# Sliding-window attention and MLP on one core: head pairs 10 and 11 moved from the early to the late kind of attention, and a new order of the first two blocks' slices

## The chip, the cores and the metric

The kernel runs on one core of a Trainium2 chip. The metric is the device time of one execution in microseconds (us); lower is better. Most executions of one kernel agree within 0.3%.

## What is computed

Attention over 4 batches of 8 heads, 768 positions and head size 64, with a band of 96 keys, 8 global keys and a distance bias; then a two-layer MLP (512 to 2048 to 512) on all 3072 tokens, in float32.

```python
scores = scale * np.matmul(q, k.transpose(0, 1, 3, 2))
is_global = pos[None, :] < int(n_global)
is_local = (rel >= 0) & (rel < int(n_local))
keep = is_global | is_local
scores = scores - slopes[:, None, None] * dist[None, :, :]
scores = np.where(keep, scores, -1000000000.0)
a = np.exp(scores - np.max(scores, axis=-1, keepdims=True))
a = a / (np.sum(a, axis=-1, keepdims=True) + 1e-09)
x = np.matmul(a, v)           # then heads side by side: 3072 x 512
h = x @ w_in
g = h * np.clip(h + 3.0, 0.0, 6.0) / 6.0
out = g @ w_out
```

## The kernel before

**Blocks, pairs, slices.** The tokens form 8 blocks of 384 (half a sequence each). A block's attention is done in 4 pairs of heads, so pair n belongs to block n // 4: pairs 0 to 3 to block 0, 4 to 7 to block 1, 8 to 11 to block 2. A block's MLP is done in 16 slices of the hidden layer (f = 0 to 15). A slice has two halves on TensorE: `first` (12 matmuls, L166, into a bank of `hp`) and `second` (9 matmuls, L198, into the block's three accumulators). Between them ScalarE adds 3 and clips below (`g`, L177), VectorE finishes the gate (L178), and the product is split into a high part (`gh`, L186 on ScalarE or L184 on GpSimd) and a rest (`gl`, L191 on VectorE). TensorE does the first half of the next slice before the second half of the last one. Each float32 product is made of three such reduced matmuls (high x high, low x high, high x low), hence 12 and 9.

**The weights** arrive as 64-bit floats, as 32 chunks of two 32-bit words each: chunk 2f holds the slice f of the first layer, chunk 2f + 1 that of the second. `decode` turns each into a high and a low part: on VectorE the steps L393, L394, L402 (merges the high word), L408 (adds the low word) and L399 (the low part, `w1l` or `w2l`); on ScalarE L371 and L412; on GpSimd L375 (`we`). Only two raw chunks fit, so the load of chunk i + 2 (L363, on SyncE's queue) is issued after L402 of chunk i. `work` gives out decode steps against a running account of TensorE time; `decoded_to` forces those that a slice needs.

**Two kinds of attention.** The early kind (`plain`) is for the time in which the weights aren't there: scores are full float32 matmuls (L809 or L813), VectorE adds the distances and takes the least (L824), ScalarE exponentiates (L828), VectorE sums and inverts (L838, L839), GpSimd normalises (L848), TensorE transposes (`turn`, L856 and L858), ScalarE or VectorE copies the transposes out (L860), and `values` multiplies (L900); `put_x` splits the result (L152 on ScalarE, L153 on VectorE). Before the change, pairs 0 to 9 have both heads side by side (`both`), and pairs 10 and 11 are still early but in a third form with one bank and operands of 128 rows. The late kind splits queries and keys (`split`: L783 on ScalarE, L784 on GpSimd, L787 and L790 on VectorE), takes scores with four reduced matmuls for each of three tiles (L813), transposes on VectorE (`spread`, L873), and carries the blocks over DRAM and back (L875 writes `there`, L882 reads `weights`, both on SyncE's queue); TensorE does only scores and `values`. The late kind is laid between the halves of a block's slices: `attention` returns a list of units, and unit k runs after the k-th half.

**Order of the work.** TensorE, GpSimd and SyncE keep the order in which the program issues (`in_order`); the other engines are put in order by the scheduler. First come pairs 0 to 11 in the loop over n, with block 0's slices 0 to 5 (`FIRST = 6`) fed in from n = 8. Then block 1's slices 0 to 5, then the slices 6 to 15 of blocks 0 and 1 in turns, all without attention beside them. From block 2 on, each block's slices carry the late attention of the block after. Block 1's sums lie in the three banks of the pools `ps_s`, `ps_t`, `ps_x`, block 0's in the three of `ps_o`.

Of the kernel before, what the change touches and what calls it, by code (L numbers as in the profile page):

```python
# [20 lines left out]
NT = 3  # L21
# [21 lines left out]
AHEAD = 3  # L43
EARLY = AHEAD * NPAIR
BOTH = 10
# [4 lines left out]
FIRST = 6  # L50
# [8 lines left out]
class Kernel:  # L59
# [222 lines left out]
    def place(self, n):  # L282
        return self.room[n % (MORE if n < EARLY else ROOMS)]

    def load(self, n, values):

        if n < len(self.blocks) * NPAIR:
            end = KW + (TB if n < BOTH else QW)
            for columns in (slice(KW + QW, LOAD),) if values else (slice(0, KW), slice(KW, end)) if n == 0 else (slice(0, end),):
                self.nc.sync.dma_start(out=self.place(n)[:, columns], in_=self.pairs[n, :, columns])  # L290

    def load_next(self, n, values):

        if n < EARLY - MORE + ROOMS:
            self.load(n + MORE, values)
        elif n >= EARLY:
            self.load(n + ROOMS, values)
# [181 lines left out]
    def banded(self, flag):  # L479
# [7 lines left out]
        self.turn, self.more, self.score_banks = {}, True, 1  # L487
# [4 lines left out]
        with ExitStack() as early, ExitStack() as words:  # L492
# [5 lines left out]
            def decoded_all():  # L498
                words.close()
                self.op = self.pool("op", 2, ctx=early, side="right")  # L500

            self.decoded_all = decoded_all
# [4 lines left out]
            with ExitStack() as ctx:  # L507
# [10 lines left out]
                def half():  # L518
                    if not self.more:
                        next(todo, None)  # L520

                for n in range(-2, EARLY + 1):
                    if n + 2 < NPAIR:
                        self.distances(n + 2)
                    if n == 8:
                        self.more = False
                        acc.extend(self.acc_tiles())
                    if n + 2 < BOTH:
# [9 lines left out]
                    for t in range(NT):  # L538
                        if n + 2 < EARLY:
                            if n + 2 < BOTH:  # L540
# [42 lines left out]
        self.score_banks = 2  # L583
        self.op = self.pool("op", 3, side="right")
        x, ahead = xs[2], None
# [30 lines left out]
    def attention(self, i, x, first):  # L616

        units = [[] for _ in range(2 * NF - 2)]
        pairs = [first or Pair(self, i * NPAIR, x, False)]
        pairs[0].x = x  # L620
        if first is None:
            for k in range(3):
                pairs[0].split(k, False)
            units[1].append(lambda: self.load_next(pairs[0].n, False))
        for p in range(NPAIR):
            n = i * NPAIR + p
            me, after = pairs[p], Pair(self, n + 1, x, False) if n + 1 < len(self.blocks) * NPAIR else None
            pairs.append(after)
            at = units[6 * p:]
            for t in range(NT):  # L630
                at[t].append(lambda t=t, me=me: me.scores(t)())
            if after:
                at[3].append(lambda after=after: after.split(0))
# [3 lines left out]
            for t in range(1, NT if after else 0):  # L637
                at[t + 3].append(lambda t=t, after=after: after.split(t))
            if p % 2 == 1:
                at[11] += [lambda me=pairs[p - 1]: me.values("x"), lambda me=me: me.values("s")]  # L640
        return units, pairs[NPAIR]
# [112 lines left out]
class Pair:  # L754
# [4 lines left out]
    def __init__(self, kernel, n, x, plain):  # L759
        self.k, self.nc, self.n, self.x, self.plain, self.both = kernel, kernel.nc, n, x, plain, n < BOTH  # L760
# [34 lines left out]
    def scores(self, t):  # L795
# [3 lines left out]
        if t != 1 or not self.both:  # L799
            self.banks = [kk.bank("s")[:, 0:2 * W].rearrange("p (i c) -> p i c", i=2) for _ in range(2 if self.both else 1)]  # L800
        sp = [self.banks[j][:, t % 2] if self.both else self.banks[0][:, j] for j in range(2)]
# [4 lines left out]
        for j in range(2):  # L806
            if self.plain:
                rows, q = (slice(j * D, (j + 1) * D), 0) if self.both else (slice(None), j)
                nc.tensor.matmul(sp[j][:, lo:W], lhsT=queries[rows, q, t], rhs=keys[rows, c], start=True, stop=True)  # L809
# [40 lines left out]
    def turn(self, t):  # L850
# [9 lines left out]
        (nc.vector.tensor_copy if kk.more and t == 1 else nc.scalar.copy)(out=pt[:, :, c], in_=tp[:, :, c])  # L860
# [61 lines left out]
def pair_loads(q, k, v):  # L922
# [8 lines left out]
    for b in range(B):  # L931
        for a in range(0, S, TB):
            cols = np.concatenate([np.arange(a - PREV, a).clip(0)]
                                  + [np.concatenate([np.arange(NG), np.arange(p, p + P)]) for p in range(a, a + TB, P)])
            for h in range(0, H, 2):
# [3 lines left out]
                for j in range(2):  # L939
                    for half in range(2):  # L940
                        if n >= EARLY or half == j:
                            column = KW + (j * TB if n >= BOTH else 0)
# [37 lines left out]
```

## Time and profile before

| What | before |
|---|---|
| median of 3 runs | 668.01 us (667.44 to 668.05) |
| the profiled execution's own time | 668.19 us |
| its span, first to last instruction | 666.4 us |
| mean granted TensorE clock | 0.999 |
| first matmul of block 0's slice 0 | at 51.55 us |
| first matmul of block 2's slice 0 (the 33rd slice) | at 202.72 us |
| VectorE busy | 423.4 us (64%) |
| ScalarE busy | 278.9 us (42%) |
| GpSimd busy | 219.9 us (33%) |
| moved by DMA | 84.74 MB |

A page of the profile gives busy time by engine over the span; the timeline gives single instructions (start, length, engine, line, operation, and in brackets the idle time before it and what ended that). On VectorE and TensorE neighbouring instructions overlap, so what one costs is read from the start of one to the start of the next. The time outside the span is 1.79 us.

### The profile page before, as it was taken

How to read it: one execution, taken by the hardware profiler on the slowest of the kernel's cores; microseconds unless marked ns; L12 is line 12 of the kernel's file. 1: busy time of each engine (PE TensorE's matmuls, PEld its weight loads, DVE VectorE, ACT ScalarE, POOL GpSimd, SP SyncE). 2: the span in 40 equal slices, each digit the busy share in tenths (PEclk: the TensorE clock that was granted, in tenths of full speed). 3: DMA queues.
4: the chain of work that ended last, by engine and by line, in shares of the span. 5: the costliest groups of instructions: out<-in, count | busy, mean ns of one | idle time of the engine just before them, and what ended most of it. 6: DMA issues, size and time to landing. Idle time of an engine off the chain costs nothing.

```text
span 666.4 us, 11474 instructions
## 1 busy us (share of the span) xinstructions
PE 654.5 (98%) x3963; PEld 586.1 (88%) x3963; DVE 423.4 (64%) x1121; ACT 278.9 (42%) x736; POOL 219.9 (33%) x389
## 2 busy tenths in 40 slices
PE   9989999999999999999999999999999999999997
PEld 8768888888999999999999999899999999989995
DVE  6899999999234876366663886457662777422222
ACT  6898756555236333154324433143331444131111
POOL 5666622221000553043340444225340444302110
PEclk9999999999999999999999999999999999999999
DMA  8685644442003446625663366624555255510001
GB/s 288 179 253 195 198 150 135 153 134 94 1 1 134 135 139 184 174 81 138 164 154 131 86 179 164 173 80 126 155 152 137 80 150 147 138 48 2 1 1 53
DMA packets 60837, 84.74 MB, mean 127 GB/s; under 512 B 8416, under 2 KB 45536, under 8 KB 60768
## 3 DMA queue, kind: packets, MB, share of 16 engines
q1 hardware_dynamic: 60480, 83.64, 43.3%
q8 instruction: 33, 0.54, 0.3%
q14 instruction: 36, 0.29, 0.1%
q10 hardware_dynamic: 288, 0.26, 0.1%
HBM read 62.92 MB, written 20.97 MB: 126 GB/s over the span
## 4 chain that ended last, share of the span: by engine, by line
PE 81%; DVE 9%; ACT 3%; DMA 3%; issue 2%; POOL 1%; SPq 0%; ACTq 0%; DVEq 0%; POOLq 0%
PE hp L166 36%; PE acc L198 33%; DMA wst<-w 3%; PE xp L900 2%; PE sp L813 2%; PE tp L900 2%; PE tp L813 2%; ACT n L828 2%; DVE wz L402 2%; DVE wz L408 1%; DVE n L824 1%; DVE wz L394 1%; PE sp L198 1%; PE tp L198 1%; PE xp L198 1%
## 5 line engine op out<-in xcount | busy, mean ns | idle before, releaser
L177 ACT ACTIVATE g<-hp,small 128x384 f32<-128x384 f32 x127 | 73.5, 579 | 251.5 <-PE hp L166 231.9
L166 PE MATMUL hp<-xh,w1h 128*128 128x384 f32 x512 | 174.1, 340 | 0.8 <-ACT w1h L412 0.7
L166 PE MATMUL hp<-xh,w1l 128*128 128x384 f32 x512 | 172.9, 338 | 0.1
L166 PE MATMUL hp<-xl,w1h 128*128 128x384 f32 x512 | 172.0, 336 | 0.0
L184 POOL TENSOR_SCALAR gh<-g 128x384 fp32r<-128x384 f32 x96 | 51.6, 538 | 292.6 <-DVE g L178 257.4
L198 PE MATMUL acc<-w2h,gl 128*128 128x512 f32 x336 | 133.0, 396 | 0.1
L198 PE MATMUL acc<-w2l,gh 128*128 128x512 f32 x336 | 132.4, 394 | 0.0
L198 PE MATMUL acc<-w2h,gh 128*128 128x512 f32 x336 | 132.0, 393 | 0.0
L178 DVE SCALAR_TENSOR_TENSOR g<-g,hp 128x384 f32<-128x384 f32 x128 | 69.7, 544 | 86.7 <-ACT g L177 86.5
L848 POOL TENSOR_SCALAR n<-n,sums 128x232 f32<-128x232 f32 (+1 forms) x186 | 101.7, 562 | 35.7 <-DVE sums L839 21.3
L191 DVE TENSOR_TENSOR gl<-g,gh 128x384 fp32r<-128x384 f32 x128 | 78.6, 614 | 50.0 <-POOL gh L184 45.3
L828 ACT ACTIVATE n<-n,least 128x232 f32<-128x232 f32 (+1 forms) x192 | 89.1, 466 | 45.1 <-DVE least L824 43.9
L166 PEld LDWEIGHTS hp<-xh,w1h 128*128 128x128 f32 x512 | 96.3, 188 | 6.6 <-issue 1.4
L166 PEld LDWEIGHTS hp<-xl,w1h 128*128 128x128 f32 x512 | 96.2, 188 | 3.9
L166 PEld LDWEIGHTS hp<-xh,w1l 128*128 128x128 f32 x512 | 96.0, 188 | 0.4 <-DVE w1l L399 0.4
L198 PEld LDWEIGHTS acc<-w2h,gl 128*128 128x128 f32 x336 | 63.0, 187 | 14.7 <-DVE gl L191 1.0
L198 PEld LDWEIGHTS acc<-w2h,gh 128*128 128x128 f32 x336 | 63.3, 188 | 10.3 <-POOL gh L184 0.3
L198 PEld LDWEIGHTS acc<-w2l,gh 128*128 128x128 f32 x336 | 63.2, 188 | 10.3
L873 DVE STREAM_TRANSPOSE blocks<-n 128x256 f32<-128x256 f32 x112 | 43.5, 424 | 31.0 <-POOL n L848 18.7
L375 POOL TENSOR_SCALAR we<-wst 128x512 int32<-128x512 uint32 x32 | 27.8, 868 | 68.6 <-DMA wst<-w 52.2
L784 POOL TENSOR_SCALAR kx<-load 64x504 fp32r<-64x504 f32 (+1 forms) x40 | 31.0, 776 | 37.5 <-PE hp L166 35.9
L824 DVE CUSTOM_DVE_ANT_0 n<-sp,d 128x232 f32<-128x232 f32 (+1 forms) x70 | 23.6, 374 | 29.5 <-PE sp L813 29.0
(110 smaller groups left out, 780.9 us busy)
## 6 DMA issues: line engine op xcount, KB each, us to landing
wst<-w SPq DMA_DIRECT2D x32, 512.0 KB, 3.5
load<-pairs SPq DMA_DIRECT2D x22, 636.0 KB, 5.2
there<-blocks SPq DMA_DIRECT2D x52, 256.0 KB, 2.6
load<-pairs SPq DMA_DIRECT2D x32, 384.0 KB, 3.9
weights<-there SPq DMA_DIRECT2D x48, 192.0 KB, 3.8
out<-o SPq DMA_DIRECT2D x23, 256.0 KB, 2.1
weights<-there SPq DMA_DIRECT2D x32, 160.0 KB, 3.2
load<-pairs SPq DMA_DIRECT2D x9, 444.0 KB, 3.6
```

What stands on the lines that cost most here:

```text
L166: self.nc.tensor.matmul(hp, lhsT=self.w1(w, f)[:, kt, :], rhs=a[:, kt, :], start=(n == 0), stop=(n == 3 * NKT - 1))
L177: nc.scalar.activation(out=g, in_=hp, func=AF.Relu, bias=self.three, scale=1.0)
L178: nc.vector.scalar_tensor_tensor(out=g, in0=g, scalar=6.0, in1=hp, op0=ALU.min, op1=ALU.mult)
L184: self.nc.gpsimd.tensor_scalar(out=gh, in0=g, scalar1=1.0, scalar2=0.0, op0=ALU.mult, op1=ALU.add)
L191: self.nc.vector.tensor_tensor(out=gl, in0=g, in1=gh.bitcast(F32), op=ALU.subtract)
L198: self.nc.tensor.matmul(acc[tt], lhsT=a[:, tk], rhs=self.w2(w, f), start=(f == 0 and j == 0), stop=(f == NF - 1 and j == 2))
L375: self.nc.gpsimd.tensor_scalar(out=self.e[i], in0=words[:, :, 0].bitcast(U32), scalar1=2.0 ** -29, scalar2=0.0, op0=ALU.mult, op1=ALU.add)
L784: nc.gpsimd.tensor_scalar(out=part["kx"][own, c], in0=k[own, c], scalar1=1.0, scalar2=0.0, op0=ALU.mult, op1=ALU.add)
L824: nc.vector.tensor_tensor_reduce(out=e[:, j, lo:W], in0=sp[j][:, lo:W], in1=d, op0=ALU.add, op1=ALU.min, scale=scale, scalar=3.0e38, accum ...
L828: nc.scalar.activation(out=e[:, j, lo:W], in_=e[:, j, lo:W], func=AF.Exp, bias=self.least[:, i:i + 1], scale=-1.0, accum_out=self.sums[:, ...
L848: nc.gpsimd.tensor_scalar(out=e[:, j, lo:W], in0=e[:, j, lo:W], scalar1=over, scalar2=0.0, op0=ALU.mult, op1=ALU.add)
L873: nc.vector.transpose(out=blocks[:, :, s].rearrange("p b j q -> p j b q"), in_=e[:, :, c:c + P].rearrange("p j (b q) -> p j b q", b=4))
```

## The change

Three things are changed together.

1. The early kind ends at pair 9 (`EARLY = 10`), and its third form is gone. Pairs 10 and 11 get the late kind. They are laid beside block 1's slices 8 to 15, with the new argument `begin`, in which a pair takes 5 units where it otherwise takes 6, and the two pairs' `values` come at unit 15, after the second half of block 1's slice 14. Their scores and values use the banks of `ps_o` (stage "one"), which block 0 leaves.
2. Of block 0, 3 slices (`FIRST = 3`) are in the loop of the early attention, not 6. The rest follows in the order of the string `ORDER`, a digit for a slice's block: 13 slices of block 0 (3 to 15) among 8 of block 1 (0 to 7), so that block 0 is done before block 1's slice 8 has its second half.
3. The loads follow: pairs from 10 on are loaded into two places, with an index shifted by one.

```diff
-EARLY = AHEAD * NPAIR
-BOTH = 10
+EARLY = 10
-FIRST = 6
+FIRST = 3
+ORDER = "101001010010010100100"
...
     def place(self, n):
-        return self.room[n % (MORE if n < EARLY else ROOMS)]
+        return self.room[n % MORE if n < EARLY else (n + 1) % ROOMS]
...
-        pools = {"s": (s, o, o, o), "t": (t, h, h), "x": (x,)}[what] if self.more else {"s": (s, t)[:self.score_banks], "t": (t,), "x": (x,)}[what]
+        pools = {"attention": {"s": (s, o, o, o), "t": (t, h, h), "x": (x,)}, "both": {"t": (t,), "x": (x,)},
+                 "one": {"s": (o,), "x": (o,)}, "layers": {"s": (s, t), "t": (t,), "x": (x,)}}[self.stage][what]
...
                         if n + 2 < EARLY:
-                            if n + 2 < BOTH:
-                                weigh[t]()
-                            else:
-                                pairs[n + 2].scores(t)()
-                                if t == NT - 1:
-                                    self.load_next(n + 2, False)
-                            self.work(0 if n + 2 < BOTH else 0.78, 0.64)
+                            weigh[t]()
+                            self.work(0, 0.64)
...
-            todo = [(1, f, xs[1], acc1) for f in range(FIRST)]
-            todo += [(i, f, xs[i], (acc, acc1)[i]) for f in range(FIRST, NF) for i in range(2)]
+            next_f, todo = [FIRST, 0], []
+            for block in map(int, ORDER):
+                todo.append((block, next_f[block], xs[block], (acc, acc1)[block]))
+                next_f[block] += 1
             for _ in self.halves(todo):
                 pass
+            self.decoded_to(2 * NF - 1)
...
+        self.stage = "one"
+        units, ahead = self.attention(2, xs[2], Pair(self, EARLY, xs[2], False), True)
+        for k, _ in enumerate(self.halves([(1, f, xs[1], acc1) for f in range(next_f[1], NF)], True)):
+            for unit in units[k]:
+                unit()
+        self.stage = "layers"
...
-            at = units[6 * p:]
+            at = units[5 * p + 1 if begin else 6 * p:]
...
-            if p % 2 == 1:
-                at[11] += [lambda me=pairs[p - 1]: me.values("x"), lambda me=me: me.values("s")]
+            if n % 2 == 1:
+                at[9 if begin else 11] += [lambda me=pairs[p - 1]: me.values("x"), lambda me=me: me.values("s")]
```

On VectorE, where the early attention ends, these rows stood after pair 8's normalisation was prepared: L838 and L839 are pair 9's sums, L824 pair 10's distances, L402, L408 and L399 the decode of chunk 3, L178 slice 0's gate.

```order
L838 TENSOR_SCALAR sums<-sums 128x6
L824 ISA n,least<-sp,p_176 128x128
L824 ISA least 128x1
L824 ISA n,least<-sp,p_176 128x128
L824 ISA least 128x1
L839 RECIPROCAL sums<-sums 128x6
L402 SCALAR_TENSOR_TENSOR wz<-wst,wz 128x512
L153 TENSOR_TENSOR xl<-xp,xh 128x384
L408 ISA wz<-wz,we 128x1024
L178 SCALAR_TENSOR_TENSOR g<-g,hp 128x384
```

The same place on VectorE after the change (the line numbers are one lower from L165 on).

```order
L837 TENSOR_SCALAR sums<-sums 128x6
L402 SCALAR_TENSOR_TENSOR wz<-wst,wz 128x512
L838 RECIPROCAL sums<-sums 128x6
L152 TENSOR_TENSOR xl<-xp,xh 128x384
L408 ISA wz<-wz,we 128x1024
L177 SCALAR_TENSOR_TENSOR g<-g,hp 128x384
L399 TENSOR_TENSOR w2l_143<-wz,w2h_142 128x512
L393 TENSOR_SCALAR wz<-wz 128x512
L190 TENSOR_TENSOR gl<-g,gh 128x384
```

Pair 10's distances are gone from between them, as pair 11's are a little later, and the decode steps move up.

On TensorE, at the end of block 1 in the program before, block 1's last second half (into `sp`, `tp`, `xp`) follows the first half of block 2's slice 0, and then come the scores of pair 12.

```order
L198 MATMUL tp<-w2h_1393,gl 128x512
L198 MATMUL xp<-w2h_1393,gh 128x512
L198 MATMUL xp<-w2l_1394,gh 128x512
L198 MATMUL xp<-w2h_1393,gl 128x512
L813 MATMUL sp<-kx,q_2409 128x232
L813 MATMUL sp<-kx,q_2410 128x232
```

After the change, at the same place on TensorE: the second half of block 1's slice 14, then the values of pairs 10 and 11, then the first half of block 2's slice 0.

```order
L197 MATMUL xp<-w2h_1102,gl 128x512
L899 MATMUL acc<-weights,load_73 64x128 x10
L899 MATMUL acc<-weights,load_72 64x128 x10
L165 MATMUL hp<-xh,w1h_140 128x384
L165 MATMUL hp<-xl,w1h_140 128x384
```

Block 2's last two value products now stand directly ahead of the first matmuls that read block 2's `x`.

More of the change, by code (lines that the diff above doesn't have):

```diff
@@ L518, in half @@
                 def half():
-                    if not self.more:
+                    if self.stage == "both":
                         next(todo, None)
@@ L632, in attention @@
             if after:
-                at[3].append(lambda after=after: after.split(0))
+                at[2 if begin else 3].append(lambda after=after: after.split(0))
             at[3] += [me.sum_up, lambda me=me: me.normalize(0), lambda me=me: me.normalize(1)]
@@ L637, in attention @@
             for t in range(1, NT if after else 0):
-                at[t + 3].append(lambda t=t, after=after: after.split(t))
-            if p % 2 == 1:
-                at[11] += [lambda me=pairs[p - 1]: me.values("x"), lambda me=me: me.values("s")]
-        return units, pairs[NPAIR]
+                at[t + (2 if begin else 3)].append(lambda t=t, after=after: after.split(t))
+            if n % 2 == 1:
+                at[9 if begin else 11] += [lambda me=pairs[p - 1]: me.values("x"), lambda me=me: me.values("s")]
+        return units, pairs[-1]
     def general_setup(self):
@@ L807, in scores @@
             if self.plain:
-                rows, q = (slice(j * D, (j + 1) * D), 0) if self.both else (slice(None), j)
-                nc.tensor.matmul(sp[j][:, lo:W], lhsT=queries[rows, q, t], rhs=keys[rows, c], start=True, stop=True)
+                rows = slice(j * D, (j + 1) * D)
+                nc.tensor.matmul(sp[j][:, lo:W], lhsT=queries[rows, 0, t], rhs=keys[rows, c], start=True, stop=True)
             else:
```

51 lines of the change are left out of this document (23 added, 28 removed).

## Prediction

> **What bounds the kernel now.** I read the page first, then busy time in stretches, then the chain of waits, then the timelines of TensorE and VectorE up to 166 us. The page:
>
> ```profile
> span 666.4 us, 11474 instructions
> PE 654.5 (98%) x3963; PEld 586.1 (88%) x3963; DVE 423.4 (64%) x1121; ACT 278.9 (42%) x736; POOL 219.9 (33%) x389
> ```
>
> TensorE is the bound on the average. The stretches (start and end; then busy us of PE, PEld, DVE, ACT, POOL; clock; DMA share; GB/s) tell where something else is close:
>
> ```profile
> 51.00:78.00 27.00, 26.19 (x188) 23.17 (x189) 25.87 (x69) 22.48 (x61) 18.47 (x26) 1.00 0.63 198
> 78.00:97.00 19.00, 17.39 (x115) 14.80 (x115) 17.55 (x34) 11.07 (x21) 4.79 (x5) 1.00 0.52 165
> 97.00:162.40 65.40, 65.31 (x326) 58.27 (x325) 64.76 (x122) 38.71 (x67) 16.29 (x18) 1.00 0.41 137
> ```
>
> From 51 to 162 us VectorE (DVE) is as full as TensorE (PE): the rows sum to 108.2 of 111.4 us, against 108.9. It decodes the weights there. After 97 us TensorE hardly waits for that, because the program before gives it slices of block 1 that need no new weights. So the change meets two full engines, and I count both and take the later. The chain gives what a slice costs, what the late kind adds to TensorE, and a mark at 165.16 us:
>
> ```profile
> 160.96 2.12 PE hp L166 x12
> 165.16 2.10 PE hp L166 x12
> ...
> 311.07 0.39 PE sp L813 x4
> 313.58 0.45 PE tp L813 x4
> 316.13 0.44 PE sp L813 x4
> 322.85 1.25 PE xp L900 x20
> 324.10 1.10 PE tp L900 x20
> ```
>
> A slice is 165.16 - 160.96 = 4.20 us, a half 2.1. A late pair of a sequence's first half, as 10 and 11 are, takes 0.39 + 0.45 + 0.44 = 1.28 us for scores, and two such pairs 2.35 us for values: 4.9 us for both. The mark is the 24th first half, since of the matmuls that occur four times in a slice 92, for 23 slices, begin before it:
>
> ```profile
> L166 PE MATMUL hp<-xl,w1h x92: 334/337/342, 51.8 to 162.6; 128*128 128x384 f32 x92
> ```
>
> **The change, part by part.** *TensorE up to the mark.* The 24th first half follows 3 + 20 slices now (it is the last digit of `ORDER`, block 0's slice 15), 6 + 17 before. Nothing differs up to about 51 us. From there:
>
> ```profile
> 51.55 0.45 PE L166 MATMUL hp<-xh,w1h 128*128 128x384 f32 x1
> 53.77 0.95 PE L809 MATMUL sp<-load 128*128 128x232 f32 x4
> 54.55 0.27 PE L856 MATMUL tp<-ident,n 128*128 128x128 f32 x1
> 55.08 1.54 PE L900 MATMUL xp<-pt,load 128*64 128x128 f32 x24
> 56.55 1.05 PE L809 MATMUL sp<-load 128*128 128x232 f32 x4
> ```
>
> From start to start: a first half 2.2 us, a tile's scores 0.78, four transposes 0.5, values 1.47; a second half is 2.1 as above. Out go pairs 10's and 11's six tiles of scores (4.7 us), their transposes and their values, and three slices are put off. Left are 3 first halves (6.6), 2 second (4.2), five groups of transposes (2.5 at most, one of them half as long) and the values of pairs 7 to 9 (4.4 at most): 17.0 to 17.7 us. So block 1's first slice can begin at 68.5 to 69.2 us and the mark, 20 slices of 4.20 later, at 152.5 to 153.2 us as far as TensorE goes.
>
> *VectorE up to the mark.* The mark needs chunk 30, whose last step is the fourth row here:
>
> ```profile
> 52.92 0.17 DVE L838 TENSOR_SCALAR sums<-sums 128x6 f32<-128x6 f32 x1
> 127.17 0.55 DVE L178 SCALAR_TENSOR_TENSOR g<-g,hp 128x384 f32<-128x384 f32 x1
> 127.63 0.69 DVE L408 CUSTOM_DVE_ANT_0 wz<-wz,we 128x1024 uint16<-128x1024 uint16 x1
> 162.38 0.68 DVE L399 TENSOR_TENSOR w1l<-wz,w1h 128x512 fp32r<-128x512 f32 x1
> ```
>
> And these are groups of the 65.0 us from 97.3 to 162.3:
>
> ```profile
> L408 DVE CUSTOM_DVE_ANT_0 wz<-wz,we 128x1024 uint16<-128x1024 uint16 x18 | 15.0, 836 | 0.3
> L191 DVE TENSOR_TENSOR gl<-g,gh 128x384 fp32r<-128x384 f32 x16 | 9.7, 604 | 0.0
> L178 DVE SCALAR_TENSOR_TENSOR g<-g,hp 128x384 f32<-128x384 f32 x15 | 8.1, 543 | 0.0
> ```
>
> A gate takes 127.63 - 127.17 = 0.46, say 0.47, and I give a rest as much; 31 of them 14.6; so each of 18 chunks takes (65.0 - 14.6) / 18 = 2.80 us. In the new order, from 52.92 us to chunk 6's last step: 3.5 chunks (9.8), three gates and rests (2.8), three splits of `x` of a gate's size (1.4), sums and their like (1.1): 68.0 us. From there to chunk 30's: 24 chunks (67.2), 20 gates and rests (18.8), one split (0.5): 154.5 us. The mark can begin 0.3 us later, since only its third matmul reads that low part: 154.8. Pairs 10's and 11's work on VectorE is gone from this count. It has no idle time but that after 97 us; from 51 to 97 us VectorE idled 27.00 - 25.87 + 19.00 - 17.55 = 2.6 us in the rows above. The decode still has one load on its way per chunk, so I keep half, 1.3 us: 156.1 us. VectorE is the later by some 3 us, and TensorE will wait about that much for weights, which it hardly does now after 97 us. The mark comes 165.16 - 156.1 = 9.1 us earlier.
>
> *After the mark* the slices are the same in number. Added is the late work of two pairs, 4.9 us on TensorE, with nothing to hide it. Its part on VectorE (splits, distances, transposes) comes behind the last chunk, so it delays no weights. On SyncE's queue block 0's three stores now stand ahead of pair 12's load and of pair 10's `there`, and no weight load is left behind them.
>
> *A new wait.* Pair 11's values stand 7 halves, one score group and pair 10's values behind the start of its last scores: 14.7 + 0.45 + 1.25 = 16.4 us. By then its blocks must have been over DRAM. Two pairs of this form before: the start of their last scores, their reads' issue on SyncE's queue, and from issue to landing (least, median, most):
>
> ```profile
> 288.21 0.61 PE L813 MATMUL sp<-kx,q 128*128 128x232 f32 x4
> 302.71 1.76 SPq L882 DMA_DIRECT2D weights<-there  x4
> DMA to landing us min/median/max: 2.6/3.3/3.9
> ...
> 302.09 0.61 PE L813 MATMUL tp<-kx,q 128*128 128x232 f32 x4
> 314.70 1.73 SPq L882 DMA_DIRECT2D weights<-there  x4
> DMA to landing us min/median/max: 2.6/3.2/3.6
> ```
>
> The last of four reads is issued about 1.3 us after the first (three quarters of 1.76): landed at 302.71 + 1.3 + 3.9 = 307.9, or 314.70 + 1.3 + 3.6 = 319.6, that is 19.7 or 17.5 us after the scores began. These pairs have 6 units each and time enough; with 5, TensorE stands for 1.1 to 3.3 us, and queued behind are block 2's first half and all the rest. I take 1.7, nearer to the second, a pair that is the odd one of its two as 11 is. [...] The banks that blocks 0 and 1 leave to scores cost some tenths, since a store's scaling ends about when the second half does: 0.3 in all, 0 to 1.
>
> *The sum*: -9.1 + 4.9 + 1.7 + 0.3 = -2.2 us on the span. The profiled execution took 668.19, so 666.0 from it; the median of the runs lies 0.18 lower and gives 665.8 us.
>
> **The rivals.** *The decode goes slower than counted, and the kernel with it (slower).* Weights landed late where pair loads ran beside them:
>
> ```profile
> 74.43 4.64 DMA wst<-w
> 83.42 3.42 DMA wst<-w
> ```
>
> The new order asks for chunks 5 to 10 sooner. If each of the ten chunks from 4 on loses half of the 1.22 us between these two, that is 6 us of idle VectorE: 671.9 us. It decides from 2.2 us of such idle time on. For it: VectorE's idle time from 78 to 97 us. Against: no pair's load but part of pair 11's is left for that time (its values), and by the counts the decode leads at chunk 6 (68.0 us, wanted only two halves after 68.5).
>
> *Pair 11's blocks are later still.* At the 19.7 us of the first pair the wait is 3.3 us, and with a microsecond more for the stores on the queue 4.3: 668.4 us, no change.
>
> *GpSimd sets VectorE free, and TensorE stays the bound.* Beside POOL's `we` VectorE's merges take longer:
>
> ```profile
> 73.48 0.68 DVE L402 SCALAR_TENSOR_TENSOR wz<-wst,wz 128x512 int32<-128x512 int32 x1
> 81.76 1.14 DVE L402 SCALAR_TENSOR_TENSOR wz<-wst,wz 128x512 int32<-128x512 int32 x1
> 71.47 5.09 POOL L848 TENSOR_SCALAR n<-n,sums 128x128 f32<-128x128 f32 x6 [0.17 <-ACT wz L371]
> 81.36 0.99 POOL L375 TENSOR_SCALAR we<-wst 128x512 int32<-128x512 uint32 x1 [1.47 <-DMA wst<-w]
> ```
>
> 0.46 us is lost beside 0.99 of POOL. If the normalisation of pairs 10 and 11, 5.09 us for one of them, costs VectorE at that rate, 4.7 us come free when it leaves this stretch, the mark falls to TensorE's 152.5, and the time to 662.2. Against: the merge at 73.48 ran beside such a normalisation and kept its 0.68. [...]
>
> *That the change doesn't do what it says* is no case here: the orders above show both pairs moved.
>
> **How the numbers follow.** A measurement of this kernel tells about 0.2% (1.3 us) from no change. Chances: the forecast 0.55, slow decode 0.12, late blocks 0.23, free VectorE 0.10. Within the forecast's case the mark may lie from 154.8 to 157.5 and the waits from 0.5 to 2.5; one part in six of it is within 0.2%. Faster: 0.46 + 0.10 = 0.56. Slower: most of the slow decode and a fifth of the late blocks, 0.15. Same: 0.29. The low end has the mark at 154.8 and half a microsecond of waits: 665.8 - 1.3 - 1.5 = 663.0. The high end has late blocks and 1.6 us of late weights: 668.4 + 1.6 = 670.0.
>
> **What would show it.** Right: the 24th first half at 155 to 157 us; between 69 and 156 us waits of PE for `w1h` or `w1l` of 3 to 5 us in all; VectorE full up to 157; and 1 to 3 us of idle PE ahead of the second values of L899 in `acc`, which stand near 198 us. Wrong: a mark beyond 158.3 us, which eats the gain; VectorE idle while weights are awaited; or more than 4 us in front of those values.

## The result and the profile after

The changed kernel takes 672.16 us (median of 6 runs, 671.80 to 674.87), the kernel before 668.02 in 6 runs beside it: a ratio of 1.0077, 95% interval 1.0058 to 1.0096. It is slower by 4.1 us, where the forecast was 665.8 and faster. The profiled execution took 672.15 us, near the median. A few executions, four of the kernel before and one of e10_chain, took far longer (799 to 3664 us); every ratio in this document leaves them out.

The page of the changed kernel, first the totals, then the granted clock in 40 slices of the span:

```profile
span 670.3 us, 11482 instructions
...
PE 653.7 (98%) x3943; PEld 582.6 (87%) x3943; DVE 433.5 (65%) x1139; ACT 274.9 (41%) x726; POOL 221.0 (33%) x401
...
PEclk9999999998999999999999999999999999999999
```

TensorE is a shade less busy than before (653.7 us, 654.5 before) and the span is 3.9 us longer, so TensorE waits more. One slice has an 8 in the clock, where the page before has none. The stretches (columns as before: busy us of PE, PEld, DVE, ACT, POOL; clock; DMA share; GB/s):

```profile
51.00:78.00 27.00, 26.63 (x186) 23.65 (x185) 24.32 (x48) 17.61 (x38) 9.38 (x15) 1.00 0.59 179
78.00:97.00 19.00, 18.68 (x92) 16.11 (x92) 18.73 (x36) 11.37 (x20) 4.67 (x6) 1.00 0.41 138
97.00:158.00 61.00, 58.76 (x285) 50.54 (x283) 60.44 (x113) 34.99 (x61) 12.50 (x16) 1.00 0.42 139
```

VectorE is full from 78 to 158 us, as foretold, and now TensorE is the one with gaps: 2.24 us from 97 to 158, where it had 0.09 from 97 to 162.4. What TensorE waited for from 69 to 212 us (sum, times, longest):

```profile
PE acc L899 <- DMA weights<-there: 2.9, 1, 2.9
PE hp L165 <- DVE w1l L399: 1.4, 3, 0.5
PE hp L165 <- ACT w1h L412: 1.2, 1, 1.2
```

These are the two causes of waiting that the prediction named, the decode and pair 11's blocks, and this view has no third. Two of the three waits for `w1l` stand ahead of the mark:

```profile
121.62 0.45 PE L165 MATMUL hp<-xh,w1l 128*128 128x384 f32 x1 [0.46 <-DVE w1l L399]
143.58 0.44 PE L165 MATMUL hp<-xh,w1l 128*128 128x384 f32 x1 [0.47 <-DVE w1l L399]
```

The timeline of TensorE around the mark, the 24th first half:

```profile
155.72 0.39 PE L197 MATMUL xp<-w2h,gl 128*128 128x512 f32 x1
157.30 0.44 PE L165 MATMUL hp<-xh,w1h 128*128 128x384 f32 x1 [1.19 <-ACT w1h L412]
157.58 0.34 PE L165 MATMUL hp<-xl,w1h 128*128 128x384 f32 x1
158.39 0.45 PE L165 MATMUL hp<-xh,w1l 128*128 128x384 f32 x1 [0.47 <-DVE w1l L399]
...
160.21 0.52 PE L165 MATMUL hp<-xh,w1l 128*128 128x384 f32 x1
160.53 0.52 PE L165 MATMUL hp<-xh,w1h 128*128 128x384 f32 x1
...
163.88 0.34 PE L165 MATMUL hp<-xh,w1h 128*128 128x384 f32 x1
```

TensorE stands for 1.19 us, does two matmuls, and stands for 0.47 more. Then its matmuls start 0.32 us apart, where they start 0.175 apart elsewhere. The granted clock is low there (single microseconds, columns as above):

```profile
157.00:158.00 1.00, 0.62 (x2) 0.30 (x2) 1.00 (x3) 0.24 (x1) 0.00 (x0) 1.00 0.00 0
158.00:159.00 1.00, 0.61 (x3) 0.61 (x4) 0.94 (x2) 0.00 (x0) 0.00 (x0) 0.86 0.00 0
159.00:160.00 1.00, 1.00 (x5) 1.00 (x4) 0.69 (x1) 0.20 (x1) 0.00 (x0) 0.50 0.00 0
160.00:161.00 1.00, 1.00 (x5) 1.00 (x4) 0.55 (x1) 0.41 (x1) 0.00 (x0) 0.50 0.00 0
161.00:162.00 1.00, 1.00 (x5) 0.90 (x4) 0.14 (x1) 0.21 (x1) 0.22 (x1) 0.50 0.00 0
162.00:163.00 1.00, 1.00 (x6) 0.82 (x5) 0.64 (x2) 1.00 (x3) 0.92 (x2) 0.93 0.00 0
```

The clock was halved for 3.4 us behind the gap (with 0.50 and 1.00 as its two values: 0.28 us of the row with 0.86, three whole rows, and 0.14 us of the row with 0.93). From the mark to the next first half it took 163.88 - 157.30 = 6.58 us where a slice takes 4.18 (165.00 to 169.18 us before): 0.47 of waiting, and 1.93 that I put down to the half clock (3.4 us at half speed account for 1.7 of it; behind the same gaps with a clock of 1.00 the way took 5.04 us in e1_ready below, 1.54 less). The other wait, from pair 11's last scores to block 2's first matmul on TensorE:

```profile
184.95 0.61 PE L812 MATMUL acc<-kx,q 128*128 128x232 f32 x4
...
200.13 1.32 PE L899 MATMUL acc<-weights,load 128*64 128x128 f32 x20
204.34 1.32 PE L899 MATMUL acc<-weights,load 128*64 128x128 f32 x20 [2.89 <-DMA weights<-there]
205.59 0.44 PE L165 MATMUL hp<-xh,w1h 128*128 128x384 f32 x1
```

Pair 11's last scores begin at 184.95 us; its values could begin at 201.45 (204.34 less the 2.89 of idling), 16.5 us later, and begin at 204.34, 19.4 us later.

**The sum of the two profiled executions.** At the 25th first half the changed kernel is 5.3 us ahead (163.88 against 169.18). From there to block 2's first matmul it takes 41.71 us against 33.54: 8.2 more, of which 2.9 are the wait and 5.3 the late work. From there to the end it takes 1.0 more. -5.3 + 8.2 + 1.0 = 3.9, the difference of the spans.

### The profile page after: what moved, and what is told of

Read it like the earlier page. It is cut to its first block, busy times and chain, and to the rows that moved or that the text cites. A ratio compares the mean times of both kernels' runs of the same rounds, so it can differ in the third digit from the quotient of the medians.

```text
span 670.3 us, 11482 instructions
## 1 busy us (share of the span) xinstructions
PE 653.7 (98%) x3943; PEld 582.6 (87%) x3943; DVE 433.5 (65%) x1139; ACT 274.9 (41%) x726; POOL 221.0 (33%) x401
## 4 chain that ended last, share of the span: by engine, by line
PE 75%; DVE 11%; DMA 5%; ACT 3%; issue 3%; POOL 1%; SPq 0%; ACTq 0%; POOLq 0%; DVEq 0%
PE hp L165 33%; PE acc L197 31%; DMA wst<-w 4%; PE tp L812 2%; PE xp L899 2%; DVE wz L402 2%; PE sp L899 2%; DVE wz L408 2%; PE sp L812 2%; ACT n L827 1%; DVE wz L394 1%; DVE wz L393 1%; DVE n L823 1%; DMA there<-blocks 1%; DVE w1l L399 1%
## 5 line engine op out<-in xcount | busy, mean ns | idle before, releaser
L165 PE MATMUL hp<-xh,w1h 128*128 128x384 f32 x512 | 174.8, 341 | 1.3 <-ACT w1h L412 1.2
L165 PE MATMUL hp<-xh,w1l 128*128 128x384 f32 x512 | 173.7, 339 | 1.4 <-DVE w1l L399 1.4
L165 PE MATMUL hp<-xl,w1h 128*128 128x384 f32 x512 | 172.6, 337 | 0.0
L183 POOL TENSOR_SCALAR gh<-g 128x384 fp32r<-128x384 f32 x104 | 56.1, 539 | 316.5 <-DVE g L177 280.7
L190 DVE TENSOR_TENSOR gl<-g,gh 128x384 fp32r<-128x384 f32 x128 | 81.2, 634 | 48.4 <-POOL gh L183 48.4
L847 POOL TENSOR_SCALAR n<-n,sums 128x232 f32<-128x232 f32 (+1 forms) x186 | 98.8, 549 | 35.8 <-DVE sums L838 22.0
L165 PEld LDWEIGHTS hp<-xh,w1h 128*128 128x128 f32 x512 | 96.6, 189 | 7.9 <-ACT w1h L412 2.2
L165 PEld LDWEIGHTS hp<-xl,w1h 128*128 128x128 f32 x512 | 96.6, 189 | 3.7
L165 PEld LDWEIGHTS hp<-xh,w1l 128*128 128x128 f32 x512 | 96.5, 188 | 2.4 <-DVE w1l L399 2.4
L197 PEld LDWEIGHTS acc<-w2h,gh 128*128 128x128 f32 x336 | 63.4, 189 | 10.6 <-ACT gh L185 0.4
L872 DVE STREAM_TRANSPOSE blocks<-n 128x256 f32<-128x256 f32 x122 | 47.5, 424 | 30.7 <-POOL n L847 18.2
L375 POOL TENSOR_SCALAR we<-wst 128x512 int32<-128x512 uint32 x32 | 24.5, 766 | 77.0 <-DMA wst<-w 68.4
L823 DVE CUSTOM_DVE_ANT_0 n<-tp,d 128x232 f32<-128x232 f32 (+1 forms) x70 | 23.7, 375 | 31.6 <-PE tp L812 31.3
L783 POOL TENSOR_SCALAR kx<-load 64x504 fp32r<-64x504 f32 (+1 forms) x44 | 34.0, 774 | 8.0 <-PE hp L165 5.7
```

The lines of the kernel that those rows point to most:

```text
L165: self.nc.tensor.matmul(hp, lhsT=self.w1(w, f)[:, kt, :], rhs=a[:, kt, :], start=(n == 0), stop=(n == 3 * NKT - 1))
L183: self.nc.gpsimd.tensor_scalar(out=gh, in0=g, scalar1=1.0, scalar2=0.0, op0=ALU.mult, op1=ALU.add)
L190: self.nc.vector.tensor_tensor(out=gl, in0=g, in1=gh.bitcast(F32), op=ALU.subtract)
L197: self.nc.tensor.matmul(acc[tt], lhsT=a[:, tk], rhs=self.w2(w, f), start=(f == 0 and j == 0), stop=(f == NF - 1 and j == 2))
L783: nc.gpsimd.tensor_scalar(out=part["kx"][own, c], in0=k[own, c], scalar1=1.0, scalar2=0.0, op0=ALU.mult, op1=ALU.add)
L823: nc.vector.tensor_tensor_reduce(out=e[:, j, lo:W], in0=sp[j][:, lo:W], in1=d, op0=ALU.add, op1=ALU.min, scale=scale, scalar=3.0e38, accum ...
```

## The experiments

My theory after the result: the loss is made of two waits on TensorE's path, the decode at the mark (with a half clock behind it) and the trip of pair 11's blocks; the rest of the sum stands. The rivals: the late work itself costs more than counted; the new order costs something by itself; the clock falls for reasons of its own. The measured times, with the kernel before on the same chip:

| Kernel | median us | before | ratio, 95% interval |
|---|---|---|---|
| e1_ready | 670.01 | 667.87 | 1.0039 (1.0024 to 1.0054) |
| e2_lean | 676.82 | 667.87 | 1.0131 (1.0113 to 1.0149) |
| e3_both | 672.59 | 667.87 | 1.0077 (1.0058 to 1.0096) |
| e4_before_lean | 675.53 | 667.87 | 1.0119 (1.0101 to 1.0138) |
| e5_spin | 673.04 | 668.42 | 1.0069 (1.0055 to 1.0084) |
| e6_nine | 674.36 | 668.42 | 1.0089 (1.0076 to 1.0102) |
| e7_finish | 669.67 | 668.42 | 1.0022 (1.0013 to 1.0031) |
| e8_nine_finish | 669.75 | 668.42 | 1.0018 (1.0006 to 1.0030) |
| e9_order | 668.65 | 668.44 | 1.0007 (0.9997 to 1.0017) |
| e10_chain | 669.42 | 668.44 | 1.0014 (1.0004 to 1.0025) |
| e11_chain_nine | 667.65 | 668.44 | 0.9993 (0.9984 to 1.0002) |
| e12_best | 667.17 | 668.24 | 0.9987 (0.9977 to 0.9997) |

**e1_ready: the trip taken off the path.**

```diff
+        if self.n < 3 * NPAIR:
+            return self.k.ident[0:K, :]
         return self.weights[0:K, :, t, 1 - c, j]
```

> The changed kernel, but the values of pairs 10 and 11 multiply a constant tile, so they don't wait for the blocks that come back over DRAM; the transfers are still made. It leaves out the attention weights of these two pairs in that product. Theory (the trip of pair 11's blocks stands on TensorE's path): the 2.9 us of idle TensorE ahead of the last values are gone, block 2's first slice starts at about 202.6 us, and the time is 672.2 - 2.9 = 669.3 us. Rival (the wait only shows there; something else, such as the split of x or block 2's banks, ends just as late): TensorE stands right behind instead, and the time stays above 671.5 us.

670.01 us, 2.2 below the changed kernel where 2.9 were expected; in the profiled execution (667.38 us) both pairs' values run without a gap and block 2 follows:

```profile
198.87 2.42 PE L901 MATMUL acc<-ident,load 128*64 128x128 f32 x40
201.22 0.45 PE L165 MATMUL hp<-xh,w1h 128*128 128x384 f32 x1
```

So the wait was on the path, and nothing else held TensorE there for long. In this execution the same 1.20 and 0.47 us of gap stood at the mark, and the clock behind it stayed at 1.00: its 25th first half follows the mark 5.04 us later, not 6.58. The half clock is not certain after such a gap.

**e2_lean and e4_before_lean: less work on VectorE.** The same edit, in the changed kernel and in the one before:

```diff
-                ts(out=z.bitcast(F32), in0=z.bitcast(F32), scalar1=LEAST, scalar2=MOST, op0=ALU.max, op1=ALU.min)
+                if i < 6:
+                    ts(out=z.bitcast(F32), in0=z.bitcast(F32), scalar1=LEAST, scalar2=MOST, op0=ALU.max, op1=ALU.min)
```

> The changed kernel without the decode's clamp (the step on L393) from chunk 6 on, which leaves out the treatment of weights of extreme size; 26 steps of 0.48 us less on VectorE. Theory (VectorE's decode sets the mark, the 24th first half, and the gap in front of it brings the half clock): the mark falls to TensorE's count, 152.5 to 153.5 us, no stretch of lower clock follows, the 25th first half starts at about 157.0 instead of 163.9, and with pair 11's wait as it was the time is 665.3 us (664.5 to 666.5). Rival 1 (the loads of raw weights or GpSimd set the pace of the decode, not VectorE's work): the mark stays beyond 156 us and the time above 671 us. Rival 2 (the clock falls by itself): the mark moves but the clock still falls for some 3 us after 150 us, and the time is 667 to 668 us.

> Control: the kernel before without the clamp from chunk 6 on, which leaves out the same treatment of extreme weights. Theory (before the change TensorE waits for weights only ahead of 97 us, 0.8 us from 51 to 78 and 1.6 from 78 to 97): it gains between 0 and 2.4 us, 665.6 to 668.0, far less than the 6.9 us of the changed kernel. Rival (less VectorE work helps any order, for instance by contention): it gains as much as the changed kernel, 661 to 662 us.

Both became slower, by 4.7 and 7.7 us, which neither theory nor rival had. The decode did what was expected of it: in the changed kernel without the clamp chunk 30's last step begins at 147.04 us, 10.6 earlier, and TensorE no longer waits for a weight. But the mark came at 163.15 us, later than 157.30, because TensorE now waits for the gates' products `gh` and `gl` (the longest of TensorE's waits from 51 to 212 us, then the chunk's last step in VectorE's timeline):

```profile
PE acc L900 <- DMA weights<-there: 2.8, 1, 2.8
PE sp L197 <- DVE gl L190: 2.7, 4, 0.7
PE sp L197 <- ACT gh L185: 2.3, 2, 2.1
PE acc L197 <- DVE gl L190: 1.6, 3, 0.7
```

```profile
147.04 0.68 DVE L400 TENSOR_TENSOR w1l<-wz,w1h 128x512 fp32r<-128x512 f32 x1
```

The scheduler that orders VectorE drew the shorter decode steps forward: the 20th slice's gate stands behind 31 finished chunks in this kernel's order, behind 26 in the changed kernel's. What VectorE saved it spent ahead of gates. So the edit changed two things at once: it shows that the decode's pace is mostly VectorE's work (rival 1 falls, since the loads were the same), but it gives no price for the mark. That took edits that leave the decode's steps as they are (below).

**e3_both.**

> Both edits together: no clamp from chunk 6 on, and the values of pairs 10 and 11 on a constant tile; it leaves out these two parts. Theory (the two losses are separate and stand one after the other): the gains add up, 6.9 + 2.9, to 662.4 us. Rival (the late work itself costs TensorE more than the 4.9 us counted, and waits come back elsewhere): above 664.5 us.

672.59 us; against e2_lean 4.2 less, so the trip's wait can be taken away on its own here as well, and no wait for weights or for pair 11's blocks is left in its profile. The 10.2 us above the expected 662.4 I put down to the gates' lateness, as in e2_lean; no run separates it.

**e5_spin: the gap at the mark filled with work.**

```diff
-    def first(self, f, x):
+    def first(self, f, x, spins=0):
...
+        any_ = self.three.broadcast_to([P, P])
+        for _ in range(spins):
+            self.nc.tensor.matmul(hp[:, 0:P], lhsT=any_, rhs=any_, start=True, stop=True)
...
-            g = self.gate(self.first(f, x), block == len(self.blocks) - 1 and f == NF - 1)
+            g = self.gate(self.first(f, x, 5 * (block == 0 and f == NF - 1)), block == len(self.blocks) - 1 and f == NF - 1)
```

> The changed kernel with five small matmuls of a constant (128x128, some 0.23 us each) put on TensorE into the result bank ahead of the mark's first half, so that TensorE works through most of the 1.19 us in which it waits for the weights of block 0's slice 15; the bank is overwritten afterwards. Theory (the half clock for some 3 us behind the mark comes from that gap): the mark stays at 157.3 us, the clock behind it stays at 1.00, and the time is 672.2 - 1.9 = 670.3 us with a mean clock of 0.999. Rival (the clock's fall has another cause; it was absent in the profiled execution of the kernel whose pairs 10 and 11 read a constant, behind the same gap): clocks of 0.992 to 0.997 remain, and the time is 672.2 within 0.5 us.

673.04 us: no gain, so the theory's number fails, and the rival's 672.2 within 0.5 is missed as well. Its profile shows a full pace behind the filled gap, and a half clock behind the other one (the timeline, with line numbers 3 higher, then the clock):

```profile
156.48 1.27 PE L164 MATMUL hp<-small 128*128 128x128 f32 x10
157.63 0.45 PE L168 MATMUL hp<-xh,w1h 128*128 128x384 f32 x1
...
202.93 1.94 PE L902 MATMUL acc<-weights,load 128*64 128x128 f32 x20 [2.56 <-DMA weights<-there]
```

```profile
203.00:204.00 1.00, 1.00 (x15) 1.00 (x17) 0.00 (x0) 0.00 (x0) 0.00 (x0) 0.73 0.18 63
204.00:206.00 2.00, 2.00 (x13) 1.67 (x10) 0.56 (x1) 0.48 (x1) 0.00 (x0) 0.50 0.15 18
```

Behind the filled gap TensorE's matmuls start 0.176 us apart (six of them, from 159.01 to 159.89 us), where the changed kernel had 0.32; 2.56 us of gap and the half clock behind it stayed at the other place, and the median does not show the difference. Two of its six runs had a mean clock of 1.00, where the profiled one with its half clock has 0.997, and still took 671.06 and 673.59 us. The half clock is thus not the whole of the loss, and why the median did not fall is open.

**e6_nine, e7_finish, e8_nine_finish: the two waits taken away by order alone.**

```diff
-ORDER = "101001010010010100100"
+ORDER = "1010010100100101001010"
...
-            at = units[5 * p + 1 if begin else 6 * p:]
+            at = units[4 * p + 1 if begin else 6 * p:]
...
-at[9 if begin else 11] += [lambda me=pairs[p - 1]: me.values("x"), lambda me=me: me.values("s")]
+at[8 if begin else 11] += [lambda me=pairs[p - 1]: me.values("x")] + [self.finish] * begin + [lambda me=me: me.values("s")]
```

In e6_nine and e8_nine_finish the last tile of the next pair is split a unit sooner as well, and where block 1's last second half moves, block 2's late attention keeps its places. The first two of these changes and the unit 8 are e6_nine, `self.finish` (with unit 9) is e7_finish, all of it e8_nine_finish.

> The changed kernel with a ninth slice of block 1 ahead of block 0's slice 15 (the string is then 1010010100100101001010) and the late pairs laid in steps of 4 units where they had 5, with the values at unit 13, so that the last scores of pair 11 stand as many halves ahead of its values as they did. Nothing is left out, and TensorE has the same work. Theory (the mark is set by VectorE's decode at 157.65 us): one more slice of TensorE work and one more gate and rest on VectorE come ahead of it, TensorE arrives at 160.3 and the weights at 158.6 us, the gap of 1.66 us and the half clock behind it (1.9 us) are gone, pair 11's wait stays near 2.9 us, and the time is 672.2 - 3.6 = 668.6 us. Rival (tighter steps make the late scores wait for split keys, or the wait for weights moves to the slices before): the time stays above 670.5 us.

> The changed kernel with block 1's last second half between the values of pair 10 and those of pair 11, where it came after block 2's first half. Nothing is left out. Theory (pair 11's blocks land 2.9 us late): they get 2.1 us more, the wait is 0.8 us, and the time is 672.2 - 2.1 = 670.1 us. Rival (the last second half waits for its own gate there, or block 2's first slice for the split of pair 11's values, and TensorE stands as long): above 671.5 us.

> The ninth slice ahead of the mark and block 1's last second half between the two values, together. Nothing is left out. Theory (two separate waits on TensorE's path): the gains add, 672.2 - 3.6 - 2.1 = 666.5 us, below the kernel before at 668.0. Rival (the late work on TensorE is dearer than counted): above 668.0 us.

e7_finish came as expected, 669.67 us for 670.1, with the wait at 0.9. e6_nine came out 5.8 us above its 668.6, and I had miscounted: with steps of 4 the last scores of pair 11 stand 6 halves ahead of its values, not 7. The mark's part of it is right (the first matmul of block 0's slice 15, now the 25th first half, 3.64 us earlier than 163.88 and with no wait, while the last step of chunk 30 begins on VectorE at 158.01), and the other wait has grown (TensorE's timeline, then the clock):

```profile
160.24 0.34 PE L165 MATMUL hp<-xh,w1h 128*128 128x384 f32 x1
...
196.14 0.50 PE L197 MATMUL sp<-w2h,gl 128*128 128x512 f32 x1 [0.84 <-DVE gl L190]
...
203.35 2.40 PE L899 MATMUL acc<-weights,load 128*64 128x128 f32 x20 [4.07 <-DMA weights<-there]
```

```profile
203.00:204.00 1.00, 0.65 (x6) 0.68 (x8) 0.00 (x0) 0.00 (x0) 0.00 (x0) 0.50 0.39 151
204.00:209.00 5.00, 5.00 (x28) 4.67 (x25) 0.56 (x1) 0.48 (x1) 0.00 (x0) 0.50 0.32 82
```

A gap of 4.07 us goes with 6.8 us of half clock, which begins inside it, at about 202.5, and ends at 209.3. In e8_nine_finish that gap is 2.33 us with 3.4 us of half clock, and 1.33 us were lost to a late rest ahead of it; what the mark gave was spent there.

**e9_order: the order alone.** The kernel before, with pairs 10 and 11 early:

```diff
-            todo = [(1, f, xs[1], acc1) for f in range(FIRST)]
-            todo += [(i, f, xs[i], (acc, acc1)[i]) for f in range(FIRST, NF) for i in range(2)]
+            next_f, todo = [FIRST, 0], []
+            for block in map(int, "101010101010100100" + "1" * 8):
+                todo.append((block, next_f[block], xs[block], (acc, acc1)[block]))
+                next_f[block] += 1
```

> The kernel before with the order alone changed: all twelve pairs early and block 0's six slices in the loop as before, then block 0's slices 6 to 15 among block 1's first eight, so that block 0's slice 15 is the 24th first half as in the changed kernel, then block 1's other eight. Nothing is left out. Theory (the order costs nothing by itself; the loss comes because TensorE gets further ahead by the pairs' removal than VectorE's decode does): VectorE has chunk 30 at 162.4 us, TensorE wants it at 165, no wait, and the time is 668.2 us within 0.7. Rival (finishing block 0 first is what makes TensorE wait for weights): 1 us or more of waits for w1h and w1l between 97 and 170 us, and over 670 us.

668.65 us against 668.44: no difference that this measurement tells. Chunk 30's last step begins at 161.77, TensorE wants it at 165.29, and TensorE has one wait from 97 to 212 us:

```profile
PE hp L166 <- DVE w1l L399: 0.6, 1, 0.6
```

```profile
161.77 0.68 DVE L399 TENSOR_TENSOR w1l<-wz,w1h 128x512 fp32r<-128x512 f32 x1
...
165.29 0.34 PE L166 MATMUL hp<-xh,w1h 128*128 128x384 f32 x1
```

Finishing block 0 first costs nothing that these runs show. What is left as the cause of the wait at the mark is the pairs' removal, which puts TensorE further ahead than VectorE.

**e10_chain, e11_chain_nine, e12_best: pair 11's blocks sooner.** The splits of pair 12 go behind pair 11's sums, and some of pair 11's normalisation to VectorE. e10_chain stands on e7_finish, the other two on e8_nine_finish; e12_best reads

```diff
-                at[2 if begin else 3].append(lambda after=after: after.split(0))
+                at[5 * p if begin and p else 2 if begin else 3].append(lambda after=after: after.split(0))
...
-            if self.n == 0:
+            if self.n == 0 or self.n == EARLY + 1 and t < 2:
                 nc.vector.tensor_scalar(out=e[:, j, lo:W], in0=e[:, j, lo:W], scalar1=over, scalar2=None, op0=ALU.mult)
```

> The kernel with block 1's last second half ahead of pair 11's values, and pair 11's blocks made sooner as well: the splits of pair 12 come two units later, behind pair 11's sums on GpSimd and VectorE, and the normalisation of pair 11's first tile is on VectorE, not on GpSimd. Nothing is left out. Theory (what is left of the wait, 0.9 us, hangs on the time from pair 11's last scores to the reads): the blocks land 2 us sooner or more, the wait is gone, and the time is 669.7 - 0.9 = 668.8 us. Rival (VectorE, with that work in front of its gates, makes TensorE wait for the gate's rest, as it did 1.3 us with the ninth slice): 669.7 us or more.

> The same two edits and the ninth slice of block 1 ahead of block 0's slice 15 with steps of 4 units. Nothing is left out. In the kernel with the ninth slice the last scores of pair 11 turned out to stand six halves ahead of its values, not seven, so its wait grew by one half, and that hid the gain at the mark. Theory (mark and trip are both waits on TensorE's path, and the half clock follows on either): with the blocks 2 us sooner the wait falls from 2.3 us to 0.3 or less, no clock falls, and the time is 669.75 - 2.0 - 0.8 = 667.0 us, below the kernel before. Rival (the ninth slice only trades the wait at the mark for later ones): 668.8 us or more, as the kernel without it.

> The last kernel (ninth slice ahead of the mark, block 1's last second half between the two values, pair 11's blocks made sooner) with two more steps on the same chain: the splits of pair 12 come one more unit later, so that none of them stands between pair 11's sums and its last transposes, and the normalisation of pair 11's first two tiles is on VectorE. Nothing is left out. Theory (in the profile of that kernel GpSimd's kx of pair 12, 1.30 us, and VectorE's, 1.83 us, stand ahead of pair 11's last transposes, and the wait left is 2.1 us with 1.7 us of half clock behind it): the wait is under 0.3 us, no clock falls, and the time is 670.2 (the profiled execution of that kernel) - 2.1 - 1.7 = 666.4 us, 0.3% below the kernel before. Rival (the wait that is left hangs on the transfers, or the gates wait behind the added work on VectorE): 667.5 us or more.

669.42, 667.65 and 667.17 us. e10_chain lost its 0.9 us of wait, but the median moved only by 0.25, within the intervals, so its runs decide between neither theory nor rival. e11_chain_nine gained 2.1 on e8_nine_finish of the 2.8 expected, and its profiled execution, the slowest of its 11 at 670.18, still has 2.1 us of wait with 3.4 us of half clock. Against e10_chain, which differs in little but the ninth slice ahead of the mark that it lacks, it is 1.8 us faster, and the two intervals do not touch: that is what the runs give as the price of the mark, and the rival's 668.8 or more fails. e12_best misses its 666.4 by 0.8, between theory and rival; its profiled execution (666.26), one of its fastest, has

```profile
PE hp L165 <- DVE w1l L399: 0.9, 2, 0.5
PE tp L855 <- POOL n L847: 0.6, 1, 0.6
PE acc L899 <- DMA weights<-there: 0.6, 1, 0.6
```

and a full clock throughout TensorE's work. Its median is 5.0 us below the changed kernel's and 0.13% below the kernel before (0.03 to 0.23%): with the two waits all but gone the loss is gone, and a gain is left that is barely clear of noise. That is not the prediction's sum come true. The forecast of 2.2 us below counted 1.7 us of wait that this kernel hardly has, and by the medians the gain is 1.1.

## Why the prediction was wrong

**TensorE up to block 1's first slice: right.** 68.5 to 69.2 us was counted, 68.46 measured. From there to the mark it was not: 20 slices of 4.20 would have brought TensorE there at 152.5, but its last matmul ahead of the mark starts at 155.72. About 3.5 us went in small pieces on low parts of weights (the rows at 121.62 and 143.58 us) and on rests and other late operands. VectorE thus set the pace well ahead of the mark, and the waits for weights came to 2.6 us in all, where 3 to 5 were to show the forecast right.

**VectorE up to the mark: the count of work right, the idle time too small.** The step that failed is "so I keep half, 1.3 us". VectorE idled 2.68 + 0.27 = 2.95 us from 51 to 97 us (the stretches above), 2.6 before; what it idles after 97 us is already in the 2.80 us of a chunk. 154.5 of counted work and 2.95 of idling make 157.45, and chunk 30's last step stood at 157.65. I halved the idle time without a row that says why it should fall. Its largest part has a cause that the change leaves alone (VectorE's waits from 51 to 160 us; then an instance, on ScalarE and on VectorE):

```profile
DVE wz L393 <- ACT wz L371: 1.9, 4, 1.0
```

```profile
75.49 0.67 ACT L371 ACTIVATE wz<-wst 128x512 f32<-128x512 f32 x1 [1.99 <-DMA wst<-w]
...
76.19 0.43 DVE L393 TENSOR_SCALAR wz<-wz 128x512 f32<-128x512 f32 x1 [0.97 <-ACT wz L371]
```

A raw chunk lands, ScalarE takes its absolute value, and VectorE waits for that; the kernel keeps two raw chunks at most, and this came back four times. Before the change it cost 2.1 us in the same place. The mark came at 157.30 us, not 156.1. It began 0.35 us ahead of that last step, where the forecast had it 0.3 behind, and its third matmul then waited.

**What the wait at the mark does: the larger miss there.** The step that failed is to take the mark's place as the whole price ("The mark comes 165.16 - 156.1 = 9.1 us earlier"), with nothing for what stands behind it. Behind it stood 0.47 us for the low part and 1.93 us that I put down to the half clock in this execution, so at the next first half the lead was 5.3 us, not 9.1. The mark also kept short of 158.3, from which on I had called the forecast wrong, and the gain was gone all the same. The profile before shows no half clock amid its work: its rows of single microseconds stand at 1.00 up to 664 us. Here it lasted 3.4 us behind gaps of 1.19 and 0.47 us; in other kernels it lasted 3.4 us with gaps of 2.14 to 2.56 us and 6.8 us with one of 4.07 us, and behind the gaps of 1.20 and 0.47 us in e1_ready there was none. What sets it off is not shown.

**The late work: right.** 4.9 + 0.3 counted, 8.17 - 2.89 = 5.3 measured.

**The new wait: right mechanism, wrong size.** The 16.4 us from scores to values were 16.5. The landing was put at 18.1, "nearer to the second, a pair that is the odd one of its two as 11 is"; it was 19.4, like the first pair's 19.7. So the term was 2.9 us, not 1.7. In the changed kernel pair 12's splits stand on VectorE and GpSimd ahead of and between pair 11's sums, normalisation and last transposes; moving them behind, with one tile's normalisation moved to VectorE, took away the 0.9 us that e7_finish had left (e10_chain). Which of the two edits did it is not shown.

**After block 2's first matmul: 1.0 us not foreseen.** Some 0.3 of it is at the first late scores (210.04 us), which wait for a bank that ScalarE is storing from (`tp`, from 209.39 to 209.99 us); the rest comes in tenths over the later blocks, and I have not found its cause.

Put together: 1.2 and 0.2 (the chain's row for the mark before stands 0.16 us behind its first matmul) and 0.47 and 1.93 at the mark, 1.3 between it and block 2, 1.0 behind: 6.1 us between the forecast from the profiled execution, 666.0, and 672.15.

**The rivals.** Late weight loads: half true. VectorE's waits behind them were about as long as before (1.9 us, 2.1 before), so the idle time stayed; 2.95 us of it against the 1.3 that I allowed is 1.65, short of the 2.2 from which that rival decides. GpSimd's leaving did not free VectorE: its merges on L402, by which that rival goes, took 693 ns from 51 to 158 us, 724 before, and those on L408 811 and 786, so the two together did not change. Pair 11's blocks came later than taken, as that rival has it, though that alone would have been no change. What no rival had is that a half clock, here of 3.4 us, can stand behind a wait, and that the wait at the mark has a second part. By the runs, taken as differences to the kernel before beside each, the trip's wait is worth 2.0 us (e1_ready) to 2.9 (e7_finish), and the mark 1.8 (e11_chain_nine against e10_chain). That each gap's half clock comes from the gap is argued from the profiles and not shown by an experiment: the profiles of the changed kernel, e5_spin, e6_nine, e8_nine_finish and e11_chain_nine show a half clock amid the work, and e2_lean's timeline the pace of one, each with a gap of 1.66 to 4.07 us, and no row of single microseconds of the kernel before, the changed kernel, e8_nine_finish, e9_order, e10_chain, e11_chain_nine and e12_best shows one elsewhere from 20 us to TensorE's last matmul, but filling one gap did not lower the median (e5_spin).

## What to carry to other kernels

When work is taken from the front of a stage with two full engines, count both and let the idle time of the second stay as it is unless its cause goes; the smaller of the two gains is all that came here (the mark 165.16 - 157.30 = 7.9 us earlier, where TensorE's count alone gave 165.16 - 152.5 = 12.7). The wait of 2.9 us that this change added on TensorE was worth 2.0 to 2.9 us, and such waits had, in some of these profiles, 3.4 or 6.8 us of half clock with them, so it is worth a different order of the same work to have none. An edit that only shortens steps can move the order that a scheduler makes, and then it is not the experiment that it seems.

## What the runs showed of the hardware

By the rows of single microseconds the granted clock stood at 0.50 for 3.4 us with gaps of TensorE of 1.66 us (the changed kernel, in two pieces, within 2.3 us), 2.14 (e11_chain_nine), 2.33 (e8_nine_finish) and 2.56 us (e5_spin), and for 6.8 us with a gap of 4.07 us (e6_nine). In e2_lean, behind a gap of 2.81 us, TensorE went at the same half pace from 207.76 to 214.10 us, 6.3 us. Behind gaps of 1.67 us in e1_ready and 1.69 in e7_finish (each in two pieces) and 2.89 us in the changed kernel the clock stayed at 1.00, and behind 2.06 us in e2_lean the matmuls of 512 columns were 0.23 us apart again within a microsecond, as at full clock, so the length of a gap alone does not decide. A matmul of 384 columns starts 0.32 us after the one before it at half clock and 0.175 at full (the changed kernel, 158.93 to 161.17 us and 163.88 to 164.92 us).
